# Reordering the head of a fused sketch-attention and routed expert kernel: pair numbers behind row scatters, batch 2's first work ahead of the first expert block

## Chip, cores and metric

The kernel runs on one core of a Trainium2 chip. The metric is the device time of one execution in microseconds (us), the median over the runs. A profile of one execution gives the durations. Five queues matter: PE (TensorE, with its weight loads shown as PEld), DVE (VectorE), ACT (ScalarE), POOL (GpSimd) and SP (SyncE, which here only issues transfers).

## What is computed

The reference has two stages. Attention with a polynomial sketch for 4 batches, 4 heads, 1088 tokens and head size 32, and then a mixture of 8 experts of which each of the 4352 tokens takes two.

```python
def phi(x):                                   # 64 features per head
    a = np.einsum('rd,bhsd->bhsr', S1, x)
    b = np.einsum('rd,bhsd->bhsr', S2, x)
    return np.einsum('bhsi,bhsj->bhsij', a, b).reshape(*x.shape[:-1], r * r)
q_p, k_p = (phi(q), phi(k))
kv = np.einsum('bhsf,bhsd->bhfd', k_p, v)     # state of a batch
z = np.sum(k_p, axis=2)
num = np.einsum('bhsf,bhfd->bhsd', q_p, kv)
den = np.einsum('bhsf,bhf->bhs', q_p, z)[..., None] + 1e-06
x = num / den                                 # then tokens x 128

logits = x @ w_gate
noisy_logits = logits + np.log1p(np.exp(x @ w_noise)) * noise
top2 = np.argpartition(-noisy_logits, 2, axis=1)[:, :2]
# softmax over the two, then for each expert e and rank k:
h = np.maximum(x[mask] @ w1[e], 0.0)          # 128 -> 1024
out[mask] += top2_w[mask, k, None] * (h @ w2[e])
```

## The kernel before

**Attention.** A batch is cut into 8 tiles of 128 tokens and a rest of 64 tokens; the rests of two batches share one tile. `Features` makes the 64 features of four tiles. `turn` transposes the inputs on PE and ACT copies them out (`xT`); `sketch` multiplies with the sketch on PE and ACT copies half of it out (`ab`); `multiply` is two DVE instructions, the second of which (`phi`, 1.23 us) is the outer product. `keys_values` accumulates the state `kv` of a batch over its key tiles in one PSUM bank; `through_router` passes that state through the gate weights (transposes, then a small product), so that the routing logits come out of the same product as the numerators. `Attend` transposes the query features (`phT`) and multiplies them with the state (`nd`).

**Routing.** `router` is a chain of some forty small DVE instructions for one batch (batch 0 is done in two halves, `h0` and `h1`, all later ones at once), with an exponential, a logarithm and another exponential on ACT in between. It ranks each token's two experts, counts with three small matmuls on PE (`side`, lines 564 to 566) how many pairs go before it, and ends with the row numbers `to` and with the rows `xg`, 128 values and one pair number each. The pair numbers are copied into `xg` by POOL (line 585); the 128 values are four DVE products (line 589). Then POOL sends the rows of 128 tokens at a time to a table in HBM (`xs`) by an indirect transfer (line 606): sixteen for batch 0, eighteen for batch 1. `xg` has two buffers. For batch 0 all rows are sent at once; later batches put theirs on a list (`waiting`), of which each expert block sends a few behind its own result.

**Expert blocks.** `table` works out on DVE which expert and which row each block of 128 pairs has: nine blocks from batch 0, then eighteen from batch 1, and so on, 72 in all with some spare at the end. `work_off` runs the blocks. SP loads a block's weights `w1` three blocks ahead and its rows `xb` two blocks ahead. The rows of a block wait for every scatter of the batches up to its own, and SP, PE, ACT, DVE and POOL each work their queue off in order. A block is a transpose of `xb` (line 767), eight matmuls into the hidden layer (line 821, ACT or DVE evict with the ReLU) and eight back (line 778, two half blocks later); POOL scatters the result (`parts`, line 785). The transpose of block b + 1 stands behind the first half of block b. At the end the two partial results of every token are summed.

**The order.** PE, ACT and DVE follow an order written out by hand (`tc.manual_schedule`); POOL and SP are ordered by the framework. `first_batches` does batches 0 and 1 up to batch 1's numerators, and batch 2's keys. Then generators alternate: for every half block the main loop takes one step of `routing` or `scores`, which hold what is left of the attention: `routing(1)` fills in batch 2's state, gate product and queries, `scores(2)` its numerators and batch 3's keys. `LONE` is the number of steps of `routing(1)` that run ahead of the first block.

PSUM is eight banks: three for features (`bank`), one for small things (`side`), two for the hidden layer (`hp`) and two for block results (`acc`). `early_bank` lets batches 0 and 1 use the last four as well, ahead of the blocks.

Of the kernel before, what the change touches and what calls it, by code (L numbers as in the profile page):

```python
# [21 lines left out]
def kernel(  # L22
# [310 lines left out]
    class Features:  # L333
# [7 lines left out]
        def turn(self):  # L341
            ps = early_bank(self.b, self.stream)
            for i, x in enumerate(self.tiles):
                nc.tensor.transpose(ps[:, P * i:P * (i + 1)], x, ident[:])  # L344
            self.xT = work.tile([P, 512], F32, name="xT", tag=f"xT{self.stream}")
            nc.scalar.copy(self.xT[:, 0:P * self.n], ps[:, 0:P * self.n])  # L346

        def sketch(self):
            n, ps = self.n, early_bank(self.b, self.stream)
# [63 lines left out]
        nc.scalar.copy(kv[RR:2 * RR, :, DH + 1:KC], both[RR:2 * RR, :, 2 * DH - 1:W])  # L413
        yield

    def through_router(b):

        kv = kvs[b]
        ps = early_bank(b, "k")
# [5 lines left out]
        ps = early_bank(b, "k")  # L425
# [48 lines left out]
    def router(nd, at_, n, t0, step, part, parts):  # L474
# [4 lines left out]
        def t3(name, w=E):  # L479
            return small.tile([P, MOST, w], F32, name=name, tag=name)[:, 0:n, :]  # L480
# [76 lines left out]
        if step == B - 1:  # L557
# [6 lines left out]
        nc.tensor.matmul(o, lhsT=earlier[:], rhs=at[0], start=True, stop=False)  # L564
        nc.tensor.matmul(o, lhsT=ones[:], rhs=so_far[:, NT - 1:NT - 1 + n, :], start=False, stop=False)
        nc.tensor.matmul(o, lhsT=ones[:], rhs=before[:].unsqueeze(1).to_broadcast([P, n, E]), start=False, stop=True)
# [5 lines left out]
        yield V.tensor_tensor(  # L572
            out=co[:, :, 0:n], in0=den.rearrange("p t a h -> p t (a h)").unsqueeze(1).to_broadcast([P, 2, n, H]),
            in1=g[:, :, 0:n].unsqueeze(3).to_broadcast([P, 2, n, H]), op=ALU.mult)
        row = t3("row")
        yield V.tensor_tensor(out=row, in0=o, in1=base[:].unsqueeze(1).to_broadcast([P, n, E]), op=ALU.add)
        of = small.tile([P, 2, MOST, E], F32, name="of", tag="of")[:, :, 0:n]
# [7 lines left out]
        nc.gpsimd.tensor_copy(xg[:, :, 0:n, D:XW].bitcast(I32), pair[:, :, t0:t0 + n].unsqueeze(3))  # L585

        for i in range(2):
            for hp in range(2):
# [7 lines left out]
                send(n)  # L596


    waiting = []

    ORDER = mybir.DependencyInfo(mybir.DependencyClass.NoSync, mybir.DependencyReason.SCHED_ONLY)

    def send(n, behind_=None):
        for _ in range(min(n, len(waiting))):
            step, i, t, to, xg = waiting.pop(0)
            x = nc.gpsimd.indirect_dma_start(  # L606
                out=xs[:], out_offset=bass.IndirectOffsetOnAxis(ap=to[:, i, t:t + 1], axis=0),
                in_=xg[:, i, t, :], in_offset=None)
            disjoint("xs", x, step)
            if behind_ is not None:  # L610
                tc.add_manual_dep(x.ins, behind_.ins.name, ORDER, reason="few at a time")

# [25 lines left out]
    def table(step, K, last):  # L638


        S_ = 3 * E if last else E
        ps = early_bank(step, "n") if step == 0 else side_bank()
        nc.tensor.matmul(ps[0:1, 0:E], lhsT=ones[:, 0:1], rhs=carry[-1][:], start=True, stop=True)
        both = const.tile([1, 2, E], F32, name=f"cnt{step}")
        if last:
# [94 lines left out]
    def work_off(*waves, skip=0, most=None, at=None):  # L740
# [68 lines left out]
            fetch_rows(i)  # L809
        acc = accumulator()  # L810
        turn_input(0, acc)
        for b in range(n):
# [58 lines left out]


    whole = slice(0, P)
    LONE = 2
    old_tokens = 3 * S - HALF
    mains = [load_batch(0)]
    load_rests(range(2), "kv")
# [32 lines left out]
    def all_of(steps_):  # L910
        for _ in steps_:
            pass
# [7 lines left out]
    def first_batches():  # L920
# [55 lines left out]
        both(8)  # L976
        p1.turn()
        p0.sketch()
        both(7)
        both(2)  # L980
        p1.sketch()
        both(3)
        all_of(h0)
        prepare(2)
        m0, m1, mr = key_parts[2]
        l0.multiply()
        m0.turn()
        l1.multiply()
        m1.turn()
        making = blocks_table(0)  # L990
        next(making)
        values = keys_values(1)
        next(values)
        next(values)
        next(values)
        all_of(h1)
        p0.multiply()
        columns = through_router(1)
        next(columns)
# [24 lines left out]

    def scores(b, nd):


        a = attends(b, nd)
# [6 lines left out]
        a[0].turn()  # L1035
        yield
        a[0].multiply()
        yield
        for f in nk:
            f.sketch()  # L1040
        for f in nk:
            f.multiply()
        yield
        a[1].turn()
        yield
        a[1].multiply()
        yield
        for x in a[2:]:
            x.turn()
            yield  # L1050
            x.multiply()
            yield

    def routing(b, nd):

# [15 lines left out]
                f.sketch()  # L1071
            yield

        filling = fill()
        for _ in steps_:
            some(steps_, 5)
            next(filling, None)
            yield
        for _ in filling:
            yield  # L1080
        making, features_ = blocks_table(b), products(nq)
        for _ in making:
            some(making, 7)
            some(features_, 2)
# [12 lines left out]
        return work_off(*[(b, WAVES[b], b > 1, WAVES[b]) if b < B - 1 else (b, LAST, True, OLD) for b in bs], **part)  # L1097

    with tc.manual_schedule(engines={PE, ACT, DVE}):
        nd = first_batches()  # L1100
        steps_ = routing(1, nd)
        some(steps_, LONE)
        needs = [0]
        blocks = block_work(*range(B), most=-SPARE, at=needs)

        def go_on():
            if needs[0] < len(tabs):
# [2 lines left out]
        for _ in steps_:  # L1110
            go_on()
        for b in (2, 3):
            nd = numerators()
            for x in (scores(b, nd), routing(b, nd)):
                for _ in x:
                    go_on()
        for _ in ends(tabs[-1], LAST):
# [45 lines left out]
```

## Time and profile before

| | us |
|---|---|
| median of 3 runs | 391.84 (390.15 to 396.99) |
| the profiled execution | 381.7 |
| its span, first to last instruction | 379.8 |
| PE busy | 352.2 (93%) |
| DVE busy | 153.7 (40%) |
| ACT busy | 126.0 (33%) |
| POOL busy | 153.3 (40%) |
| mean granted PE clock | 0.971 of full |

The profile's page gives busy time by engine and by fortieths of the span; the timelines give each instruction with its start, its length, and in brackets the idle time before it and what ended it. The profiled execution is shorter than the median of the timed runs, so sums over the profile are compared with its own 381.7 us.

### The profile page before, as it was taken

How to read it: one execution, taken by the hardware profiler on the slowest of the kernel's cores; microseconds unless marked ns; L12 is line 12 of the kernel's file. 1: busy time of each engine (PE TensorE's matmuls, PEld its weight loads, DVE VectorE, ACT ScalarE, POOL GpSimd, SP SyncE). 2: the span in 40 equal slices, each digit the busy share in tenths (PEclk: the TensorE clock that was granted, in tenths of full speed). 3: DMA queues.
4: the chain of work that ended last, by engine and by line, in shares of the span. 5: the costliest groups of instructions: out<-in, count | busy, mean ns of one | idle time of the engine just before them, and what ended most of it. 6: DMA issues, size and time to landing. Idle time of an engine off the chain costs nothing.

```text
span 379.8 us, 9206 instructions
## 1 busy us (share of the span) xinstructions
PE 352.2 (93%) x3022; PEld 344.2 (91%) x3022; DVE 153.7 (40%) x490; ACT 126.0 (33%) x310; POOL 153.3 (40%) x205
## 2 busy tenths in 40 slices
PE   8897883999999999999999999999999999998880
PEld 7886773999999999999999999999999999998880
DVE  5759849245364440287302232322223222343230
ACT  2353340355543555544442212222221222221210
POOL 7001854058762286564655546323232222322230
PEclk9998998599999999999999999999999999999995
DMA  6799672435416465466579766656465667898812
GB/s 187 192 306 292 187 239 68 131 99 171 157 49 205 130 184 166 139 198 152 179 193 291 215 183 211 179 183 187 163 205 164 187 173 257 297 263 245 254 46 89
DMA packets 45582, 70.38 MB, mean 185 GB/s; under 512 B 9939, under 2 KB 31060, under 8 KB 45536
## 3 DMA queue, kind: packets, MB, share of 16 engines
q1 hardware_dynamic: 40896, 60.76, 54.3%
q0 software_dynamic: 4480, 8.96, 6.7%
q8 instruction: 27, 0.44, 0.5%
q14 instruction: 19, 0.16, 0.1%
q10 hardware_dynamic: 160, 0.07, 0.1%
HBM read 57.99 MB, written 12.03 MB: 184 GB/s over the span
## 4 chain that ended last, share of the span: by engine, by line
PE 70%; DMA 15%; DVE 4%; issue 4%; POOL 4%; ACT 1%; SPq 1%; POOLq 0%; ACTq 0%
PE hp L821 29%; PE acc L778 28%; DMA parts<-y,xb 9%; POOL xs L606 3%; PE bank L407 2%; DMA xs<-xg,to 2%; PE bank L464 2%; PE acc L767 2%; PE bank L351 2%; DMA vld<-in_v_dram 2%; DMA xb<-xs 1%; POOL parts L785 1%; PE acc L464 1%; PE bank L447 1%; DMA two<-parts 1%
## 5 line engine op out<-in xcount | busy, mean ns | idle before, releaser
L821 PE MATMUL hp<-bT,w 128*128 128x128 f32 x1152 | 156.1, 279 | 1.1 <-PE acc L767 0.6
L778 PE MATMUL acc<-w,h 128*128 x1152 | 152.2, 275 | 0.0
L821 PEld LDWEIGHTS hp<-bT,w 128*128 128x128 f32 x1152 | 142.5, 195 | 2.4 <-PE acc L767 1.2
L778 PEld LDWEIGHTS acc<-w,h 128*128 128x128 f32 x1152 | 140.5, 193 | 0.0
L785 POOL DMA_INDIRECT parts<-y,xb x72 | 74.9, 1041 | 161.5 <-DVE y L736 87.3
L738 ACT ACTIVATE h<-hp 128x512 f32<-128x512 f32 x99 | 59.1, 597 | 149.4 <-PE hp L821 148.7
L606 POOL DMA_INDIRECT xs<-xg,to x68 | 70.7, 1040 | 49.3 <-DVE xg L589 29.0
L736 DVE TENSOR_SCALAR h<-hp 128x512 f32<-128x512 f32 x45 | 31.1, 692 | 121.8 <-PE hp L821 121.8
L738 ACT COPY bT<-acc 128x128 f32<-128x128 f32 x72 | 19.1, 265 | 30.8 <-PE acc L767 30.7
L767 PE MATMUL acc<-ident,xb 128*128 128x128 f32 x72 | 20.1, 279 | 6.8 <-DMA xb<-xs 6.8
L371 DVE TENSOR_TENSOR phi<-ab 128x1024 f32<-128x1024 f32 (+1 forms) x18 | 20.5, 1136 | 0.6
L736 DVE COPY y<-acc 128x128 f32<-128x128 f32 x45 | 13.1, 292 | 12.4 <-PE acc L778 12.4
L767 PEld LDWEIGHTS acc<-ident,xb 128*128 128x128 f32 x72 | 10.4, 145 | 7.5 <-DMA xb<-xs 5.6
L351 PE MATMUL bank<-sk,xT 128*128 128x128 f32 x102 | 13.8, 281 | 2.0 <-ACT xT L346 1.9
L407 PE MATMUL bank<-vld,phi 128*128 128x96 f32 x128 | 15.3, 275 | 0.0
L351 PEld LDWEIGHTS bank<-sk,xT 128*128 128x128 f32 x102 | 12.2, 191 | 3.2 <-ACT xT L346 2.8
L407 PEld LDWEIGHTS bank<-vld,phi 128*128 128x128 f32 x128 | 14.8, 192 | 0.0
L366 DVE TENSOR_TENSOR ab<-bank,ab 128x256 f32<-128x256 f32 (+1 forms) x15 | 5.6, 374 | 17.6 <-ACT ab L358 17.6
L489 DVE TENSOR_SCALAR den<-nd 128x16 f32<-128x16 f32 (+2 forms) x5 | 1.0, 206 | 25.1 <-ACT nd L467 25.0
L589 DVE TENSOR_TENSOR xg<-nd,co 128x256 f32<-128x256 f32 (+2 forms) x20 | 10.9, 607 | 0.6 <-issue 0.2
L346 ACT COPY xT<-bank 128x512 f32<-128x512 f32 (+1 forms) x15 | 7.5, 523 | 8.9 <-PE bank L344 6.6
L738 ACT COPY y<-acc 128x128 f32<-128x128 f32 x27 | 7.2, 265 | 7.6 <-PE acc L778 7.5
(184 smaller groups left out, 242.7 us busy)
## 6 DMA issues: line engine op xcount, KB each, us to landing
w<-in_moe_w_dram SPq DMA_DIRECT2D x72, 512.0 KB
xb<-xs SPq DMA_DIRECT2D x72, 64.5 KB
two<-parts SPq DMA_DIRECT2D x8, 512.0 KB
kld<-in_k_dram SPq DMA_DIRECT2D x4, 512.0 KB
qld<-in_q_dram SPq DMA_DIRECT2D x4, 512.0 KB
vld<-in_v_dram SPq DMA_DIRECT2D x8, 256.0 KB
out_dram<-two SPq DMA_DIRECT2D x8, 256.0 KB
parts<-y,xb POOLq DMA_INDIRECT x72, 3.4
```

Source lines behind the costliest of these rows:

```text
L351: nc.tensor.matmul(ps[:, P * i:P * (i + 1)], lhsT=self.xT[:, P * i:P * (i + 1)], rhs=sk[:].rearrange("p i h y -> p (i h y)"), start=True, ...
L371: yield V.tensor_tensor(out=self.phi[:, 0:n].rearrange("p t h (i j) -> p (t h) i j", i=R), in0=th[:, :, 0, :].unsqueeze(3).to_broadcast([P ...
L407: nc.tensor.matmul(ps[:, W * hp:W * (hp + 1)], lhsT=lhsT, rhs=rhs, start=(t == 0 and hp == 0), stop=(t == NT), skip_group_check=True)
L464: nc.tensor.matmul(ps[rows, c0:c0 + YC], lhsT=self.phT[hp][:, P * i + rows.start:P * i + rows.stop], rhs=kv[:, hp, :], start=True, stop=True)
L589: yield V.tensor_tensor(out=xg[:, i, 0:n, 2 * DH * hp:2 * DH * (hp + 1)].rearrange("p t (h d) -> p t h d", h=2), in0=x[:, :, hp, 0:2 * (DH ...
L606: x = nc.gpsimd.indirect_dma_start(out=xs[:], out_offset=bass.IndirectOffsetOnAxis(ap=to[:, i, t:t + 1], axis=0), in_=xg[:, i, t, :], in_o ...
L736: V.tensor_scalar_max(o, i, 0.0) if relu else V.tensor_copy(o, i)
L738: nc.scalar.activation(out=o, in_=i, func=AF.Relu) if relu else nc.scalar.copy(o, i)
L767: nc.tensor.transpose(acc[:, P:2 * P], rows[i][:, 0:D], ident[:])
L778: nc.tensor.matmul(acc[:, 0:D], lhsT=h[:, P * j:P * (j + 1)], rhs=w2[:, bass.ds(FJ * e + (j0 + j), 1), :], start=(j0 + j == 0), stop=(j0 + ...
L785: sent = nc.gpsimd.indirect_dma_start(out=parts[:], out_offset=bass.IndirectOffsetOnAxis(ap=rows.pop(i)[:, D:XW].bitcast(U32), axis=0), in ...
L821: nc.tensor.matmul(hp[:, P * j:P * (j + 1)], lhsT=w1[:, P * (j0 + j):P * (j0 + j + 1)], rhs=xT[:], start=True, stop=True)
```

## The change

In `router`, the copy of the pair numbers gets an ordering edge behind the last row scatter recorded so far (`sent_rows`), and for batches 1 to 3 the three counting matmuls are issued after the five DVE instructions that follow them. In `first_batches`, batch 2's keys are transposed earlier, in an `acc` bank; batch 1's state and gate product come ahead of the rest of `h1`; the first table comes later; and batch 2's state, gate product, both query groups and the first transposes of its numerators are issued before the first block. `through_router` can take its banks from another stream. The first table's counts use the `side` bank. After the first block's input transposes, the first numerator product of batch 2 is issued (`a.pop(0).multiply()`). `routing(1)` has no attention work left to fill in, apart from one query product, and `scores` is written as one loop. `LONE` becomes 1, since `first_batches` has already run a step of `routing(1)`.

```diff
@@ router @@
+        def rank_sums():
+            nc.tensor.matmul(o, lhsT=earlier[:], rhs=at[0], start=True, stop=False)
...
+        if step == 0:
+            rank_sums()
         yield V.tensor_add(out=after[:], in0=before[:], in1=so_far[:, NT + n - 1, :])
...
+        if step > 0:
+            rank_sums()
         row = t3("row")
...
-        nc.gpsimd.tensor_copy(xg[:, :, 0:n, D:XW].bitcast(I32), pair[:, :, t0:t0 + n].unsqueeze(3))
+        numbers = nc.gpsimd.tensor_copy(xg[:, :, 0:n, D:XW].bitcast(I32), pair[:, :, t0:t0 + n].unsqueeze(3))
+        if sent_rows:
+            tc.add_manual_dep(numbers.ins, sent_rows[-1].ins.name, ORDER, reason="rows first")
@@ table @@
-        ps = early_bank(step, "n") if step == 0 else side_bank()
+        ps = side_bank()
@@ work_off @@
         turn_input(0, acc)
+        yield
@@ first_batches @@
         p0.sketch()
+        prepare(2)
+        (m0, m1, mr), (n0, n1) = key_parts[2], query_parts[2]
+        m0.turn("n")
+        turning = m1.turning("n")
+        next(turning)
         both(7)
         both(2)
         p1.sketch()
         both(3)
+        all_of(turning)
         all_of(h0)
-        prepare(2)
-        m0, m1, mr = key_parts[2]
+        m0.sketch()
+        m1.sketch()
+        values = keys_values(1)
         l0.multiply()
-        m0.turn()
+        next(values)
         l1.multiply()
-        m1.turn()
-        making = blocks_table(0)
-        next(making)
-        values = keys_values(1)
         next(values)
         next(values)
-        next(values)
-        all_of(h1)
         p0.multiply()
-        columns = through_router(1)
-        next(columns)
-        some(making, 6)
-        p1.multiply()
-        m0.sketch()
         nd = numerators()
         a0, a1, ar = attends(1, nd)
+        columns = through_router(1, "q")
+        next(columns)
+        p1.multiply()
         a0.turn()
         next(columns)
         pr.turn()
+        all_of(h1)
+        a1.turn()
+        making = blocks_table(0)
+        next(making)
         pr.sketch()
-        some(making, 6)
-        a1.turn()
         a0.multiply()
         pr.multiply()
-        all_of(making)
+        m0.multiply()
         a1.multiply()
         ar.turn()
         ar.multiply()
-        m1.sketch()
+        all_of(making)
+        values = keys_values(2)
+        next(values)
         mr.turn()
+        n0.turn("q")
+        m1.multiply()
         mr.sketch()
-        m0.multiply()
-        m1.multiply()
+        n0.sketch("q")
+        next(values)
         mr.multiply()
-        return nd
+        n0.multiply()
+        steps_ = routing(1, nd)
+        next(steps_)
+        next(values)
+        n1.turn()
+        columns = through_router(2)
+        next(columns)
+        n1.sketch()
+        next(columns)
+        nd = numerators()
+        a = attends(2, nd)
+        a[0].turn()
+        return steps_, nd, a
@@ routing @@
-        filling = fill()
+        filling = fill() if b > 1 else iter(())
...
-        making, features_ = blocks_table(b), products(nq)
+        making, features_ = blocks_table(b), products(nq[1:] if b == 1 else nq)
@@ main @@
-        nd = first_batches()
-        steps_ = routing(1, nd)
+        steps_, nd, a = first_batches()
         some(steps_, LONE)
         needs = [0]
         blocks = block_work(*range(B), most=-SPARE, at=needs)
+        next(blocks)
+        a.pop(0).multiply()
```

More of the change, by code (lines that the diff above doesn't have):

```diff
@@ L339, in __init__, with bank, turn, turning @@
             self.n = len(tiles)
-        def turn(self):
-            ps = early_bank(self.b, self.stream)
+        def bank(self, stream=None):
+            return early_bank(*((self.b, self.stream) if stream is None else (0, stream)))
+        def turn(self, stream=None):
+            for _ in self.turning(stream):
+                pass
+        def turning(self, stream=None):
+            ps = self.bank(stream)
             for i, x in enumerate(self.tiles):
                 nc.tensor.transpose(ps[:, P * i:P * (i + 1)], x, ident[:])
+            yield
             self.xT = work.tile([P, 512], F32, name="xT", tag=f"xT{self.stream}")
             nc.scalar.copy(self.xT[:, 0:P * self.n], ps[:, 0:P * self.n])
-        def sketch(self):
-            n, ps = self.n, early_bank(self.b, self.stream)
+        def sketch(self, stream=None):
+            n, ps = self.n, self.bank(stream)
             for i in range(n):
@@ L414, in keys_values, with through_router @@
         yield
-    def through_router(b):
+    def through_router(b, stream="k"):
         kv = kvs[b]
-        ps = early_bank(b, "k")
+        ps = early_bank(b, stream)
         for hp in range(2):
@@ L424, in through_router @@
         yield
-        ps = early_bank(b, "k")
+        ps = early_bank(b, stream)
         for hp in range(2):
@@ L563, in router @@
         o = ps[:, 0:n * E].rearrange("p (i e) -> p i e", e=E)
-        nc.tensor.matmul(o, lhsT=earlier[:], rhs=at[0], start=True, stop=False)
-        nc.tensor.matmul(o, lhsT=ones[:], rhs=so_far[:, NT - 1:NT - 1 + n, :], start=False, stop=False)
-        nc.tensor.matmul(o, lhsT=ones[:], rhs=before[:].unsqueeze(1).to_broadcast([P, n, E]), start=False, stop=True)
+        def rank_sums():
+            nc.tensor.matmul(o, lhsT=earlier[:], rhs=at[0], start=True, stop=False)
+            nc.tensor.matmul(o, lhsT=ones[:], rhs=so_far[:, NT - 1:NT - 1 + n, :], start=False, stop=False)
+            nc.tensor.matmul(o, lhsT=ones[:], rhs=before[:].unsqueeze(1).to_broadcast([P, n, E]), start=False, stop=True)
+        if step == 0:
+            rank_sums()
         yield V.tensor_add(out=after[:], in0=before[:], in1=so_far[:, NT + n - 1, :])
@@ L596, in router @@
                 send(n)
-    waiting = []
+    waiting, sent_rows = [], []
     ORDER = mybir.DependencyInfo(mybir.DependencyClass.NoSync, mybir.DependencyReason.SCHED_ONLY)
@@ L609, in send @@
             disjoint("xs", x, step)
+            sent_rows.append(x)
             if behind_ is not None:
@@ L811, in work_off @@
         turn_input(0, acc)
+        yield
         for b in range(n):
@@ L873 @@
     whole = slice(0, P)
-    LONE = 2
+    LONE = 1
     old_tokens = 3 * S - HALF
@@ L1016, in first_batches, with scores @@
         ar.multiply()
-        m1.sketch()
+        all_of(making)
+        values = keys_values(2)
+        next(values)
         mr.turn()
+        n0.turn("q")
+        m1.multiply()
         mr.sketch()
-        m0.multiply()
-        m1.multiply()
+        n0.sketch("q")
+        next(values)
         mr.multiply()
-        return nd
-    def scores(b, nd):
-        a = attends(b, nd)
+        n0.multiply()
[11 more added lines that the diff above has]
+        return steps_, nd, a
+    def scores(b, nd, a):
         nk = []
@@ L1034, in scores @@
             f.turn()
[L1035 to L1048, printed above, removed]
+        for i, x in enumerate(a):
             x.turn()
@@ L1052, in scores @@
             yield
+            if not i:
+                for f in nk:
+                    f.sketch()
+                for f in nk:
+                    f.multiply()
+                yield
     def routing(b, nd):
@@ L1112 @@
         for b in (2, 3):
-            nd = numerators()
-            for x in (scores(b, nd), routing(b, nd)):
+            if b > 2:
+                nd = numerators()
+                a = attends(b, nd)
+            for x in (scores(b, nd, a), routing(b, nd)):
                 for _ in x:
```

## The prediction

> **What bounds the kernel now.** I read, in this order: the page (busy time and clock by slice), the table by stage, the timelines of GpSimd and TensorE over 47 to 80 us, then those of the DMA queue and TensorE at 114 to 117 us. From about 66 us to 360 us TensorE is busy almost without a break, so the end moves with whatever TensorE loses before and inside that stretch. The slices:
>
> ```profile
> PE   8897883999999999999999999999999999998880
> ...
> PEclk9998998599999999999999999999999999999995
> ```
>
> Slices 7 and 8 (57 to 76 us) hold the one large hole in the head: work falls, then the clock does. By stage (columns: window, then busy us of PE, PEld, DVE, ACT, POOL, granted clock, DMA share, GB/s):
>
> ```profile
> 60.00:65.00 5.00, 0.13 (x2) 0.00 (x0) 4.38 (x19) 0.52 (x2) 2.15 (x3) 0.93 0.16 51
> 65.00:70.00 5.00, 4.09 (x15) 3.30 (x16) 2.69 (x13) 1.16 (x4) 0.00 (x0) 0.50 0.50 148
> 70.00:75.00 5.00, 5.00 (x27) 4.94 (x27) 0.79 (x4) 1.82 (x6) 0.00 (x0) 0.55 0.40 114
> 75.00:80.00 5.00, 5.00 (x48) 5.00 (x47) 3.76 (x8) 2.56 (x7) 1.27 (x1) 1.00 0.33 93
> ```
>
> TensorE idles for five microseconds, then works ten at half clock: 27 instructions in 70 to 75, 48 in the next five. What it waits for stands in the timelines (start, length, instruction, in brackets the idle time before it and its releaser). GpSimd:
>
> ```profile
> 47.26 0.97 POOL L606 DMA_INDIRECT xs<-xg,to  x1 [0.30 <-issue]
> 50.86 0.51 POOL L585 COPY xg<-pair 128x18 int32<-128x18 int32 x1 [2.63 <-DMA xs<-xg,to]
> 51.61 0.98 POOL L606 DMA_INDIRECT xs<-xg,to  x1 [0.24 <-POOL xg L585]
> ...
> 61.28 0.97 POOL L606 DMA_INDIRECT xs<-xg,to  x1 [0.30 <-DMA xs<-xg,to]
> ```
>
> and TensorE:
>
> ```profile
> 56.42 3.71 PE L407 MATMUL bank<-vld,phi 128*128 128x96 f32 x32
> 65.55 0.48 PE L767 MATMUL acc<-ident,xb 128*128 128x128 f32 x1 [5.42 <-DMA xb<-xs]
> ```
>
> The first block needs sixteen row scatters, one every 1.27 us on GpSimd. Between the eighth and the ninth stands batch 1's copy of pair numbers, which waits until the first eight have been read out. TensorE runs dry at 60.13 and starts the block at 65.55 (call it T0). A second place matters more for this change. Block 9 is the first that needs batch 1's eighteen rows:
>
> ```profile
> 111.96 0.97 POOL L606 DMA_INDIRECT xs<-xg,to  x1 [0.30 <-DMA xs<-xg,to]
> 114.40 0.21 POOL L585 COPY xg<-pair 128x18 int32<-128x18 int32 x1 [1.48 <-DMA xs<-xg,to]
> ```
>
> ```profile
> 114.46 0.33 SPq L763 DMA_DIRECT2D xb<-xs  x1
> ```
>
> ```profile
> 115.53 1.06 PE L778 MATMUL acc<-w,h 128*128 x8
> 116.42 0.27 PE L767 MATMUL acc<-ident,xb 128*128 128x128 f32 x1
> ```
>
> The last scatter is issued at 111.96, has landed by 114.40, the load goes out at 114.46, and TensorE transposes those rows at 116.42 with no idle time shown. It is hidden, but with next to nothing to spare.
>
> **What the Trainium skill says.** "TensorE: Matmul & The Clock Gate", Part 1, has the clock at half after at least one idle window of about 3.4 us and back after a busy one. The trace agrees on the fall (half from 64.6 us), but the return took until 74.75, three such windows; and a dip to 0.50 at 34 to 37 us followed gaps of 1.3 us only. The same page (Architectural detail) has DVE, ACT and GpSimd as strict FIFOs, which is what the copy at 50.86 shows. "SBUF — State Buffer", SBUF: two separate sides, has DVE and GpSimd exclude each other on a shared port: the scatters that took 1.63, 1.84 and 1.73 us instead of 0.97 lie beside a DVE feature product of 1.23 us. "DMA: Bandwidth & Descriptors", Anatomy of one DMA, gives about 2 us plus bytes over 436 GB/s: 2.15 us estimated for 66 KB; the trace has 2.3 to 5.4.
>
> **The change, part by part** (before's clock throughout).
>
> *Pair numbers behind the scatters.* Batch 1's copy goes behind all sixteen; the second half's small copy (0.21) takes its place. The gap falls from 3.38 us to 0.30 + 0.21 + 0.24 = 0.75, so the sixteenth scatter, its landing and the first row load come 2.6 us earlier: T0 = 62.9. The first scatter stays at 36.53: it hangs on DVE, whose order up to there is unchanged. The second half's rows are now made after the two query products (2 x 1.6 us), at about 45.6 instead of 42.4; needed at 49, so free. The first table comes behind two feature products, at about 52 instead of 49.6; the three weight loads then go out near 53 and, at before's pace (issued 50.3, DMA all but idle at 58), land near 60.5. Free, with 2 us to spare. SP's order of transfers is unchanged. The counts for this table move to the side bank, which DVE frees at about 43.5 by reading the second half's rank sums; TensorE reaches them near 45.7, so this costs nothing. Were DVE late there, batch 1's numerators would queue behind it.
>
> *Batch 2 ahead of block 0.* TensorE work moved ahead of T0: rest values 0.58, state transposes 0.22, gate product 0.41, query transposes 0.87, sketches 1.79, first numerator transposes 0.87; together 4.74. Room: batch 2's key transposes (0.87) fall into the 1.33 us wait at 31.2, batch 1's numerators start about 2.3 us earlier, and 2.8 us are left between 60.1 and 62.9. Each hop waits for ACT or DVE (about 0.5 us); adding them up I have TensorE done near 62, so the hole shrinks from 5.4 us to about 1 and the clock should hold. That spares 9.2 us at 0.51, or 4.6 us.
>
> *What this uncovers.* From T0 to the tenth row transpose TensorE took 50.87 us. Less 4.6 of clock, less 4.74 moved, plus 0.80 (batch 3's rest values and state transposes, now ahead of it): 42.3, so it wants block 9's rows at 105.2. The rows don't shrink alike. Batch 1's rank sums now stand behind block 0's second half: 0.11 + 1.76 (moved numerator) + 4 x 0.89 + waits and the rest, 8.3 us after T0, at 71.2; from the rank sums' end to finished rows it was 4.15 us (75.87 to 80.02), so they are ready near 75.4 instead of 80.0. From there GpSimd is the bound: before, first to last scatter took 80.80 to 112.93, with five block results in between. Less 1.3 us that it waited for results, plus the copy of 0.45 that now stands inside: 31.3. So 75.8 + 31.3 = 107.1, landed 108.5, rows in SBUF 1.96 later: 110.5. TensorE waits 5.3 us there. Everything behind it in TensorE's queue waits too, and on SP the next weights stand behind this load; they have a block's time (3.7 us) to arrive, as now.
>
> *Sum.* The tenth transpose comes at 110.5 instead of 116.42, 5.9 us, and 0.8 us of work is behind it: 6.7. But the hole is as long as the one removed, so I expect the clock to fall again. Bounds: one window of 3.4 us at half costs 1.7; the first hole cost 4.6. I take 3.4 for it and 0.3 for a dip in the head: net 3.0. Elsewhere (tail, 320 us) nothing changes. The profiled execution took 381.7 us (span 379.8): 378.7. The timed runs lie higher, median 391.84; I carry the difference over: 388.8. A measurement of this kernel can tell about 2%, 7.8 us, from no change.
>
> Unknown costs: DVE's seventh large product beside the scatters, 0 to 0.8 us on T0; banks held by batch 2's second queries until their product, 0 to 1; the clock, 1.7 to 4.6. I take 0, 0 and 3.4. That gives 386.9 to 391.9 for this case alone.
>
> **Rivals.**
> - *The cover holds*: rows reach block 9 in time and both holes are gone. Gain 116.42 - 105.2 + 0.8 = 12.0: 379.8. For it: the rows start 4.6 us earlier. Against: eighteen scatters and five results at 1.27 each are 29 us by themselves.
> - *Block 0 isn't earlier*: batch 2's chain of hand-overs (keys, values, table, queries, numerators) ends only near 65.5, so the change doesn't do what it says at its first place. The rows shift along: 113.1 at the tenth transpose, gain 3.3 + 0.8 - 3.4 = 0.7: 391.1. For it: eleven hand-overs in one queue. Against: DVE and ACT are a third to two thirds busy there.
> - *Slower*: batch 1's exponential stands in ACT's queue behind batch 2's numerator copies, and its rank sums in TensorE's queue behind block 0. The tenth transpose is the row-ready time plus 35.1. It decides from 78.7 on (116.42 + 0.8 - 3.4 - 35.1): at 83 the kernel takes 396.1, and 2% slower needs 86.5. Against: I have 75.4, with DVE's chain (7 us from the exponential on) done at 70.
>
> **How the numbers follow.** Likeliest 0.62 (388.8), cover holds 0.12 (379.8), block 0 not earlier 0.15 (391.1), slower 0.11 (394 to 400). 382.5 to 394.5 holds the first, the third and half of the last. Faster by over 2%: the second and a little of the first, 0.15. Slower by over 2%: over half of the last and some of the third, 0.09. Within: 0.76.
>
> **What would show it.** Right: the ninth scatter 0.75 us behind the eighth's end; first block at 62 to 64 us at clock 1.0; a wait of 4 to 6 us of TensorE on row loads near 105 to 111, GpSimd without a gap before it, and a dip of the clock behind it. Wrong: no such wait (then near 380), or the first block past 65 us, or the clock at 1.00 right through the wait (then near 385).

## Result: 3.5% slower, where no change was forecast

The changed kernel took 405.31 us (median of 4 runs, 401.66 to 406.34); the kernel before took 394.28 us beside it (4 runs, 390.15 to 396.99). The ratio is 1.035, with a 95% interval of 1.026 to 1.044. Here and below, times are medians of all runs, while a ratio leaves out runs over 1.5% slower than the fastest of their kernel, so the two need not agree to the last digit. The forecast was 388.8 us with a range of 382.5 to 394.5, so it was wrong in sign and size. The profiled execution of the changed kernel took 406.34 us, its span is 404.6.

The page, same rows as shown of before:

```profile
PE   6988759999398998998999999999999999998980
...
PEclk9999755799899999899999999999999999998995
```

and the stages (columns as above):

```profile
60.00:65.00 5.00, 4.19 (x18) 3.78 (x18) 3.07 (x13) 1.92 (x5) 0.00 (x0) 0.50 0.31 112
65.00:70.00 5.00, 5.00 (x26) 4.47 (x26) 0.00 (x0) 0.59 (x2) 0.00 (x0) 0.50 0.85 258
70.00:75.00 5.00, 4.75 (x22) 4.46 (x22) 1.19 (x4) 1.34 (x4) 0.00 (x0) 0.50 0.30 107
75.00:80.00 5.00, 4.65 (x34) 3.99 (x34) 3.71 (x9) 1.54 (x5) 0.00 (x0) 0.93 0.00 0
```

TensorE is at half clock from about 45 to 76 us, not 65 to 75. GpSimd did what was forecast: the ninth scatter starts 0.48 us behind the eighth's end (forecast 0.75), and the sixteenth has left by 57.83, against 62.25 before:

```profile
46.49 0.97 POOL L623 DMA_INDIRECT xs<-xg,to  x1 [0.30 <-issue]
47.45 0.21 POOL L600 COPY xg<-pair 128x8 int32<-128x8 int32 x1
47.94 0.98 POOL L623 DMA_INDIRECT xs<-xg,to  x1 [0.28 <-POOL xg L600]
...
56.86 0.97 POOL L623 DMA_INDIRECT xs<-xg,to  x1 [0.30 <-issue]
```

But the first block starts at 81.00 instead of 62 to 64:

```profile
81.00 0.27 PE L785 MATMUL acc<-ident,xb 128*128 128x128 f32 x1
```

The loss is in the hand-overs from TensorE to ScalarE and VectorE. TensorE's timeline, then ScalarE's, then VectorE's:

```profile
48.54 1.91 PE L455 MATMUL acc<-ident,phi 128*128 128x128 f32 x8
50.38 0.20 PE L661 MATMUL side<-carry,ones 128*1 128x8 f32 x2
50.64 0.79 PE L359 MATMUL hp<-sk,xT 128*128 128x128 f32 x2
52.70 4.16 PE L472 MATMUL acc<-kv,phT 128*128 128x98 f32 x16 [1.27 <-issue]
```

```profile
52.06 0.58 ACT L460 COPY phT<-acc 128x512 f32<-128x512 f32 x1 [1.48 <-PE hp L359]
54.19 0.58 ACT L460 COPY phT<-acc 128x512 f32<-128x512 f32 x1 [1.54 <-remote]
56.33 0.21 ACT L366 COPY ab<-hp 128x64 f32<-128x64 f32 x1 [1.55 <-remote]
59.91 0.87 ACT L475 COPY nd<-acc 128x392 f32<-128x392 f32 x2 [3.37 <-remote]
```

```profile
54.23 0.15 DVE L668 COPY cnt<-side 1x8 f32<-1x8 f32 x1 [8.56 <-remote]
```

TensorE's transposes were done at 50.45, yet ScalarE copies the second half of them at 54.19; the counts were done at 50.58 and VectorE reads them at 54.23. "remote" and "issue" say that the profile found no signal in time. The trace's own record of TensorE's semaphore stands at 54.167, 0.02 us ahead of the copy: the engine didn't dawdle, the signal came late. In this stretch, while GpSimd sends, ScalarE steps on once per 2.13 us. The last send ends at 57.83, and ScalarE takes up the numerators 2.08 us behind it, at 59.91. The same holds in the other late traces of the changed kernel: ScalarE's next copy comes 2.09 to 2.24 us behind the end of the sixteenth send.

I measured this for every hand-over: for each ScalarE or VectorE instruction that waits for TensorE and comes out of idle time, its start minus the later of the matmul's end and its own engine's previous end. In the first profile of before, 341 such hand-overs have none over 0.11 us. In this one, 24 of 339 are over 0.3 us, the longest 4.63, and 22 of the 24 have a GpSimd send inside them. Below, an execution (or chip) with hand-overs over 0.3 us late is called late, one without them punctual. The first profile of before was of an execution without late signals (381.7 us); its timed runs (390 to 397) were not like it.

### The profile page after: what moved, and what is told of

Read it like the earlier page. It is cut to its first block, busy times and chain, and to the rows that moved or that the text cites. A ratio compares the mean times of both kernels' runs of the same rounds, so it can differ in the third digit from the quotient of the medians.

```text
span 404.6 us, 9203 instructions
## 1 busy us (share of the span) xinstructions
PE 364.5 (90%) x3022; PEld 353.5 (87%) x3022; DVE 153.2 (38%) x490; ACT 124.3 (31%) x310; POOL 150.4 (37%) x205
## 4 chain that ended last, share of the span: by engine, by line
PE 73%; DMA 12%; issue 5%; DVE 3%; ACT 3%; another core or an unknown queue 2%; POOL 1%; SPq 0%; POOLq 0%; ACTq 0%
PE hp L840 28%; PE acc L796 26%; DMA parts<-y,xb 8%; PE bank L415 5%; PE acc L472 2%; PE bank L472 2%; PE acc L785 2%; DMA vld<-in_v_dram 2%; PE acc L455 1%; PE bank L359 1%; PE hp L359 1%; DMA w<-in_moe_w_dram 1%; PE bank L455 1%; DMA two<-parts 1%
## 5 line engine op out<-in xcount | busy, mean ns | idle before, releaser
L796 PEld LDWEIGHTS acc<-w,h 128*128 128x128 f32 x1152 | 142.0, 194 | 1.7 <-issue 1.7
L623 POOL DMA_INDIRECT xs<-xg,to x68 | 67.9, 998 | 53.1 <-DVE xg L606 29.0
L415 PE MATMUL bank<-vld,phi 128*128 128x96 f32 x128 | 18.1, 304 | 0.4 <-DVE ab L374 0.4
L415 PEld LDWEIGHTS bank<-vld,phi 128*128 128x128 f32 x128 | 17.5, 220 | 0.8 <-DVE ab L374 0.6
L472 PE MATMUL acc<-kv,phT 128*128 128x98 f32 (+1 forms) x72 | 12.9, 358 | 5.4 <-ACT nd L475 3.6
L472 PEld LDWEIGHTS acc<-kv,phT 128*128 128x128 f32 (+1 forms) x72 | 11.6, 255 | 6.7 <-ACT nd L475 3.8
L785 PEld LDWEIGHTS acc<-ident,xb 128*128 128x128 f32 x72 | 10.3, 144 | 3.4 <-issue 1.7
L472 PE MATMUL bank<-kv,phT 128*128 128x98 f32 (+1 forms) x72 | 9.4, 280 | 2.5 <-ACT phT L460 1.6
L472 PEld LDWEIGHTS bank<-kv,phT 128*128 128x128 f32 (+1 forms) x72 | 8.0, 185 | 3.8 <-ACT phT L460 2.6
```

The source lines that it names most:

```text
L415: nc.tensor.matmul(ps[:, W * hp:W * (hp + 1)], lhsT=lhsT, rhs=rhs, start=(t == 0 and hp == 0), stop=(t == NT), skip_group_check=True)
L472: nc.tensor.matmul(ps[rows, c0:c0 + YC], lhsT=self.phT[hp][:, P * i + rows.start:P * i + rows.stop], rhs=kv[:, hp, :], start=True, stop=True)
L623: x = nc.gpsimd.indirect_dma_start(out=xs[:], out_offset=bass.IndirectOffsetOnAxis(ap=to[:, i, t:t + 1], axis=0), in_=xg[:, i, t, :], in_o ...
L785: nc.tensor.transpose(acc[:, P:2 * P], rows[i][:, 0:D], ident[:])
L796: nc.tensor.matmul(acc[:, 0:D], lhsT=h[:, P * j:P * (j + 1)], rhs=w2[:, bass.ds(FJ * e + (j0 + j), 1), :], start=(j0 + j == 0), stop=(j0 + ...
```

## Experiments

Five sets were run, each on one chip and in one session, beside before. The chip of the first comparison is not on record. On chip 1 signals are punctual, on chips 3, 6, 7 and 15 late. "First block" is TensorE's first row transpose.

### Both kernels again, and the change taken apart (chip 1)

Edge alone: old head with

```diff
+        numbers = nc.gpsimd.tensor_copy(xg[:, :, 0:n, D:XW].bitcast(I32), ...)
+        if sent_rows:
+            tc.add_manual_dep(numbers.ins, sent_rows[-1].ins.name, ORDER, reason="rows first")
...
```

(The rest of the edit makes the list `sent_rows` and fills it.)

No edge: the changed kernel with `if False:` in place of `if sent_rows:`. The other two are before and the changed kernel as they stand.

> The kernel before, once more, with its own profile. Three theories are carried through this set. BURST: the stalls of the changed kernel (instructions of ScalarE, VectorE and TensorE that start 1.5 to 8.5 us after their operands were made, while GpSimd issues its sixteen row scatters without a break) come from the unbroken burst of scatters, so from the ordering edge on the pair numbers. ORDER: they come from the new order of the head itself (batch 2's work and a late first table in front of the first block), whatever GpSimd does. CHANCE: they strike any version in some executions; the first profile of before (381.7 us, beside timed runs of 390 to 397) was one without them. BURST and ORDER expect here a time of 380 to 397 and no wait above 1.5 us of ScalarE or VectorE on a thing that was ready, with the first block's input transpose at 65 to 67 us. CHANCE expects 390 or more with such waits visible somewhere in 36 to 62 us or in 80 to 113 us, and the first block or the tenth transpose later than 65.6 and 116.4 by 3 us or more.

> The changed kernel once more. BURST and ORDER expect 400 to 407 us with the first block's transpose again at 78 to 84 us and TensorE at half clock from about 45 to 77. CHANCE expects the places of the stalls to move by several microseconds from one execution to the next, and the first block somewhere between 63 and 84.

> Before, with the ordering edge on the pair numbers alone: the sixteen scatters become one burst, nothing else of the order changes. BURST expects stalls in 48 to 58 us like those of the changed kernel, the first block at 70 us or later, and a time 5 to 12 us above before. ORDER expects the first block about 2.6 us earlier than in before (near 63), no stalls, and a time 0 to 3 us below before. CHANCE expects no difference from before beyond its spread (390 to 397).

> The changed kernel without the ordering edge: the pair numbers of batch 1 stand again between the eighth and the ninth scatter and wait there, the new order of the head stays. BURST expects no stalls, the first block at 64 to 67 us and a time of 385 to 394, level with before. ORDER expects the same stalls as in the changed kernel, the first block at 78 us or later, and 400 to 407. CHANCE expects about the changed kernel's median, with stalls in other places.

| chip 1, before 382.02 us | us | ratio (95%) |
|---|---|---|
| before again | 381.27 | 0.999 (0.996 to 1.002) |
| changed | 377.93 | 0.992 (0.989 to 0.995) |
| edge alone | 378.77 | 0.989 (0.983 to 0.994) |
| no edge | 383.97 | 1.006 (1.003 to 1.008) |

BURST, ORDER and CHANCE all failed on the changed kernel: it is a little faster than before, and no hand-over is over 0.11 us in any of the four traces, though 136 to 145 of them have a send inside. The page and the lines of the changed kernel on chip 1:

```profile
PE   8898898999959999999999999999999999997970
...
PEclk9999999999988999999999999999999999999996
```

```profile
46.03 0.20 PE L661 MATMUL side<-carry,ones 128*1 128x8 f32 x2
```

```profile
46.26 0.15 DVE L668 COPY cnt<-side 1x8 f32<-1x8 f32 x1 [0.57 <-PE side L661]
```

```profile
63.66 0.33 PE L785 MATMUL acc<-ident,xb 128*128 128x128 f32 x1 [0.90 <-DMA xb<-xs]
```

```profile
111.09 0.45 PE L785 MATMUL acc<-ident,xb 128*128 128x128 f32 x1 [4.37 <-DMA xb<-xs]
```

The same counts are read 0.04 us after TensorE's end, the first block comes at 63.66 at full clock, and TensorE waits 4.37 us for block 9's rows at 111.09. That is the forecast's picture. What separates the two comparisons isn't the kernel: before itself takes 382.02 us here and 394.28 there. I put it down to the chip, but each chip was measured in one session only, so chip and session can't be told apart.

### A second chip, and all of batch 1's rows at once (chip 3)

```diff
-            if step == 0:
+            if step <= 1:
                 send(n)
```

in the changed kernel and in the old head with the edge.

> The kernel before in a second session. Two theories of the difference between the first comparison (before 394.28, changed 405.31) and the second (382.02 and 377.93). SESSION: in the first comparison the completion signals of TensorE reached ScalarE and VectorE late (up to 5 us after the matmul) while GpSimd issued scatters, in every execution of that session, and the changed head suffers more since eleven hand-overs stand in front of its first block; whatever session has this is 8 us or more slower for before, and shows it in the trace. LOT: both comparisons drew from the same spread, and the changed kernel simply has two modes. SESSION expects either about 382 us with no late signal, or 390 to 397 us with late signals in 36 to 62 us or 80 to 113 us. LOT expects about 382 here whatever the changed kernel does.

> The changed kernel in a second session. SESSION expects it beside before as in one of the two comparisons: 376 to 381 us where before takes 379 to 385 (ratio 0.985 to 0.998, first block at 63 to 64 us), or above 400 where before takes 390 to 397. LOT expects single executions above 400 among others near 378, beside a before of about 382.

> The changed kernel with batch 1's eighteen row scatters sent at once, ahead of the block results on GpSimd's queue. In the second session's trace GpSimd needs from 77.45 to 107.64 for them, since a result of 1.3 us stands behind every third, and TensorE waits 4.37 us for block 9's rows and then runs 6.8 us at half clock. Theory GPSIMD (the queue of scatters is the bound there): the last scatter ends near 100.5, the rows land near 104, TensorE doesn't wait, and the time falls by 5 to 8 us against the changed kernel (370 to 373 beside 378). Rival ROWS (the rows are late by the routing chain or by the load, not by the queue): the wait stays above 3 us and the time within 2 us. Rival BACK (the delayed results fill up the eight result buffers or delay the last summing): the wait goes, but the time falls by less than 3 us or rises.

> The old head with the ordering edge and with batch 1's eighteen scatters sent at once. If the new order of the head is worth something only where GpSimd isn't the bound (GPSIMD), this takes 3 to 7 us more than the changed kernel with rows first, since the old head has its rows 3 us later and leaves the hole ahead of the first block: 374 to 379. If the head's order is worth nothing by itself (rival: its gain was the ordering edge's alone), both are within 2 us of each other.

Before took 394.69 us (395.48 over all its runs there), changed 401.68 (ratio 1.015, 1.010 to 1.021), rows first 412.99 (1.042, 1.034 to 1.049), the old head with rows first 412.54 (1.045, 1.037 to 1.054). SESSION held and LOT fell: the kernel before shows late signals too, 28 of 341, 24 of them with a send inside:

```profile
99.61 0.60 ACT L738 ACTIVATE h<-hp 128x512 f32<-128x512 f32 x1 [2.42 <-PE bank L351]
102.47 0.27 ACT L738 COPY bT<-acc 128x128 f32<-128x128 f32 x1 [2.27 <-PE hp L821]
```

The transpose for the second line ended at 96.73. GPSIMD couldn't be judged here: more unbroken sends meant more late signals, the longest 10.4 us in the old head with rows first.

### The two parts on a late chip, and sends that do nothing (chip 6)

```diff
+    for t in range(16):
+        disjoint("idle", nc.gpsimd.indirect_dma_start(
+            out=idle_rows[:], out_offset=bass.IndirectOffsetOnAxis(ap=idle_to[:, t:t + 1].bitcast(U32), axis=0),
+            in_=pad[:], in_offset=None))
```

> The old head with the ordering edge on the pair numbers alone. On a chip where TensorE's signals come on time (before near 382) it took 378.77, a ratio of 0.989, and should again (0.983 to 0.994). On a chip where they come late during GpSimd's sends (before near 395): theory BURST (the unbroken burst is what hurts: each hand-over that falls into it costs up to some microseconds) expects it slower than before there, ratio 1.00 to 1.015, with hand-overs over 1 us late in 48 to 60 us, where before has few. Rival LENGTH (what hurts is how many hand-overs stand in front of the first block, so the new order of the head) expects it at or below before, 0.985 to 1.000.

> The new head without the edge. On a chip with signals on time it took 383.97, a ratio of 1.0055, and should again. On a chip with late signals BURST expects it between before and the changed kernel, 1.000 to 1.010, since the break of 3.4 us between the eighth and the ninth scatter lets signals through; LENGTH expects it at the changed kernel's own ratio or above (1.015 to 1.025).

> The changed kernel with sixteen further row scatters at the start, of a constant tile into a table that nobody reads: they need nothing and run from about 8 to 28 us, while GpSimd would be idle; nothing else is changed. Theory SEND (GpSimd's sends delay TensorE's signals on the chips that have it, wherever they stand) expects hand-overs from TensorE to ScalarE or VectorE over 0.3 us late inside 8 to 28 us, where the changed kernel has none, and a time 2 to 8 us above the changed kernel's 401.7. Rival DATA (it is the rows' own traffic, the loads beside it or the routing that delay them) expects 8 to 28 us as before and a time within 2 us. On a chip with signals on time both expect no late hand-over and within 1 us of 378.

Beside a before of 392.28 us the edge alone took 397.85 (1.012, 1.001 to 1.024) and the new head without the edge 392.62 (1.001, 0.997 to 1.004). BURST held for both; LENGTH expected no loss from the edge and at least 1.015 without it. The edge's interval reaches down to 1.001, so against LENGTH the second result is the stronger one. The idle sends (406.97 us; the changed kernel had no run on this chip) ran from 8.00 to 30.64 and made hand-overs late where they never had been. TensorE, then ScalarE:

```profile
21.84 2.85 PE L472 MATMUL acc<-kv,phT 128*128 128x98 f32 x23
25.01 1.13 PE L472 MATMUL acc<-kv,phT 128*128 128x98 f32 x8 [0.33 <-issue]
```

```profile
28.06 0.49 ACT L475 COPY nd<-acc 128x392 f32<-128x392 f32 x1 [3.10 <-PE bank L351]
32.31 0.49 ACT L475 COPY nd<-acc 128x392 f32<-128x392 f32 x1 [3.77 <-remote]
```

The last product ended at 26.15; its copy starts at 32.31, and on chip 1 the corresponding copy starts at 25.58. These sends move a constant tile that nobody reads, so DATA falls: the sends make the signals late, whatever they carry. Whether it is GpSimd's issuing or the transfers that follow wasn't separated.

### The changed kernel, rows first and idle sends side by side (chip 15)

> The changed kernel as the partner of the next two on one chip. The theory (LATE: a chip either delivers TensorE's signals late during GpSimd's sends or doesn't) expects one of two pictures and nothing between: before near 382 with the changed kernel at 0.986 to 0.997 of it and no hand-over over 0.3 us, or before at 387 to 400 with the changed kernel at 1.010 to 1.045 and twenty or so hand-overs over 0.3 us. A rival (DRIFT: the lateness comes and goes on any chip) expects a mixture within this set.

> The changed kernel with batch 1's eighteen scatters ahead of the block results. On a chip with punctual signals GPSIMD (the queue of scatters bounds block 9's rows) expects the wait of 4.4 us gone and 370 to 374 us; its rival ROWS expects the wait to stay and 376 to 379. On a late chip LATE expects 406 to 417, 2 to 4% over the changed kernel, as the burst of eighteen catches the hand-overs of the first blocks.

> The changed kernel with sixteen sends of a constant tile at 8 to 28 us into a table that nobody reads. On a chip with punctual signals LATE expects no late hand-over in 8 to 36 us and the changed kernel's time within 1 us. On a late chip it expects two to six late ones of up to 4 us there, and 1 to 6 us over the changed kernel. DRIFT expects late ones on any chip.

A late chip again: before 395.08, changed 407.25 (1.033, 1.018 to 1.048), rows first 412.36 (1.051, 1.038 to 1.063), idle sends 411.96 (1.049, 1.031 to 1.066). In the idle sends' trace hand-overs at 25 to 33 us are 1.73, 3.82 and 2.64 us late; in the changed kernel's none ahead of 45 us. The 4.7 us between the two medians lie inside overlapping intervals, so the lateness is shown and its price is not. Rows first lies 1.3% above the changed kernel, less than the 2 to 4% that LATE expected. DRIFT found no support: every trace of this set is late, as every trace of chip 1's set is punctual. A slower drift, from session to session, isn't excluded.

### One hop moved (chip 7)

In every late trace of the changed kernel the counts of the first table are 3.7 to 6.7 us late. So they were moved ahead:

```diff
         p1.multiply()
+        all_of(h1)
+        making = blocks_table(0)
+        next(making)
         a0.turn()
         next(columns)
         pr.turn()
-        all_of(h1)
         a1.turn()
-        making = blocks_table(0)
-        next(making)
```

once with the edge and once without.

> The changed kernel as the partner of the other three. On a late chip 400 to 408 us and a first block at 78 to 84 us; on a punctual one 377 to 380 and 63 to 64.

> The changed kernel with one TensorE product moved: the first table's counts are taken ahead of batch 1's numerator transposes instead of behind them; no other queue changes. Theory HOP (on a late chip the hop of the counts is the costly one, since VectorE works in order and batch 1's and batch 2's feature products stand behind it) expects the copy of the counts at 45 to 49 us instead of 54 to 60, the first block 3 to 8 us earlier and the time 3 to 8 us lower than the changed kernel's. Rival QUEUE (TensorE's signals leave one after another, and whichever comes next in the burst is as late) expects the lateness to move to another hop and the time within 3 us. On a punctual chip both expect the changed kernel's time within 1.5 us.

> The same without the ordering edge, so with the break of 3.4 us between the eighth and the ninth scatter. On a late chip HOP expects the best of the new heads, 385 to 391 where before takes 390 to 396 (a ratio of 0.985 to 1.000); QUEUE expects what the new head without the edge took beside before, a ratio of 0.997 to 1.004. On a punctual chip both expect 382 to 385, as without the edge.

> The changed kernel with batch 1's eighteen scatters ahead of the block results. On a late chip 410 to 414 us, as twice already. On a punctual chip GPSIMD expects TensorE's wait of 4.4 us for block 9's rows to vanish and 370 to 374 us; its rival ROWS expects the wait to stay, at 376 to 379.

| chip 7, before 394.47 us | us | ratio (95%) | first block |
|---|---|---|---|
| changed | 402.75 | 1.026 (1.013 to 1.039) | 78.47 |
| counts early | 402.76 | 1.027 (1.016 to 1.037) | 78.95 |
| counts early, no edge | 394.12 | 1.002 (0.998 to 1.006) | 72.41 |
| rows first | 410.15 | 1.041 (1.029 to 1.053) | 80.84 |

HOP fell. VectorE now reads the counts at once, and nothing is gained: ScalarE's copy of the numerators starts at 59.37, and in the changed kernel on this chip at 59.40. Counts early, VectorE and ScalarE:

```profile
45.66 0.15 DVE L668 COPY cnt<-side 1x8 f32<-1x8 f32 x1 [0.50 <-PE side L661]
```

```profile
51.53 0.59 ACT L460 COPY phT<-acc 128x512 f32<-128x512 f32 x1 [1.52 <-PE hp L359]
53.66 0.59 ACT L460 COPY phT<-acc 128x512 f32<-128x512 f32 x1 [1.55 <-remote]
54.14 0.22 ACT L366 COPY ab<-hp 128x64 f32<-128x64 f32 x1
59.37 0.87 ACT L475 COPY nd<-acc 128x392 f32<-128x392 f32 x2 [5.01 <-remote]
```

The lateness passes to the next hop (5.01 us), as QUEUE said. Without the edge GpSimd sends nothing from 46.91 to 50.69, and ScalarE works through the same copies in and just behind that pause:

```profile
49.35 0.59 ACT L460 COPY phT<-acc 128x512 f32<-128x512 f32 x1 [0.29 <-PE acc L455]
50.20 0.59 ACT L460 COPY phT<-acc 128x512 f32<-128x512 f32 x1 [0.27 <-PE acc L455]
...
51.40 0.49 ACT L475 COPY nd<-acc 128x392 f32<-128x392 f32 x1 [0.50 <-PE acc L472]
```

So on one chip, with one edit, the edge costs 8.6 us by the medians (402.76 against 394.12) and about 10 by the ratios. Behind the pause the lateness is back: in the same trace a copy of numerators comes 5.4 us late, at 61.40. On chip 1 the edge is worth 6.0 us (383.97 against 377.93), there in the changed head with the counts in their place.

## Why the prediction was wrong

The runs compare heads as follows. Each entry is from one trace, all punctual ones of chip 1; the late ones are of chip 3 (before), chip 6 (edge alone, no edge) and, for the changed kernel, of the first comparison and chips 3, 7 and 15.

| | first block, punctual | first block, late | span, punctual | span, late |
|---|---|---|---|---|
| before | 64.49 | 68.33 | 376.2 | 393.0 |
| edge alone | 66.07 | 75.92 | 380.5 | 399.4 |
| no edge | 67.00 | 72.62 | 382.5 | 391.9 |
| changed | 63.66 | 78.47 to 82.51 | 375.5 | 399.5 to 406.1 |

The two steps that failed are the price of a hand-over and the carry-over to the timed runs, both below.

**The scatters** were right: forecast 0.75 us between eighth and ninth, measured 0.48 and 0.61.

**The first block** was forecast at 62.9. On chip 1 it is 63.66, with TensorE's hole 0.90 us (forecast about 1), at full clock, and the weights' loads issued at 52.82 (forecast near 53). In the late traces it is 78.5 to 82.5, past the 65 us that the forecast itself named as a sign of being wrong. The step that failed there is "Each hop waits for ACT or DVE (about 0.5 us)": in the changed kernel's late traces a hop beside a send comes up to 6.7 us late, and that delay is handed down TensorE's queue to the first block (81.00 in the first of them, 18.1 us behind the forecast). The clock goes down as well. In the first late trace it is at half from 44.93, inside a wait of 2.65 us of TensorE, to 75.65 us, and eight query transposes take 1.91 us instead of the 1.04 of chip 1:

```profile
45.06 1.04 PE L455 MATMUL acc<-ident,phi 128*128 128x128 f32 x8
```

**Block 9's rows** were right on chip 1: rows finished at 76.68 (forecast 75.4), last scatter done at 107.64 (107.1), tenth transpose at 111.09 (110.5), wait 4.37 (5.3). The clock dip behind it lasts 6.8 us at half, which is the 3.4 us that were taken for it. Scatters and results follow each other there at 0.30 us; that GpSimd's queue is the bound is read from this and wasn't shown by a run, since rows first met late chips three times.

**The sum** was 378.7 for the profiled execution; on chip 1 it took 377.26, and the median gain over before was 4.1 us (forecast 3.0). That agreement is partly luck. The hole of 5.42 us and the ten us at half clock that the sum removes belong to one execution of before. In the second punctual trace of before the hole is 1.82 us, the first block comes at 64.49 at full clock, the tenth transpose at 111.56, and the span is only 0.7 us above the changed kernel's. Two slips change nothing: the three unknown costs give 387.1 to 391.8, not 386.9 to 391.9, and the half-clock stretch of before lies at 64.25 to 74.49 in the trace's own record, not at 64.6 to 74.75.

**The carry-over** is where the number broke: "The timed runs lie higher, median 391.84; I carry the difference over". That 10.1 us was treated as a constant of the measurement. It goes with late signals, and it depends on the order of the work: from punctual to late the span of before grows by 16.8 us (376.2 to 393.0), that of the changed kernel by 29.1 (375.5 to 404.6). These are single executions. By the medians before takes 10.3 to 13.5 us more on the late chips than on chip 1, and the changed kernel 23.8 to 29.3. The difference, 12.3 us by the spans and 10 to 16 chip by chip, turns a gain of some 3 to 4 into a loss of 6 to 12 (6.2, 8.3 and 12.2 on chips 3, 7 and 15), and 11.0 was first measured. It arises ahead of the first block: 17.3 us there for the changed kernel (63.66 to 81.00), 3.8 for before (64.49 to 68.33).

**Why before suffers less.** From punctual to late the first block moves by 3.8 us in before, by 9.9 with the edge alone, by 5.6 with the new order alone and by 15 to 19 with both. The number of hops alone doesn't explain it: beside the second eight scatters I count 6 and 8 of them in the two punctual traces of before and 9 in the changed kernel's. On chip 7 the pause ahead of the ninth scatter, which the edge takes away, lets the waiting signals through, and with it the first block comes at 72.41 instead of 78.95. That the new order makes each delay dearer since batch 2's chain stands in front of the first block fits the table, but was only argued.

**The rivals.** "Block 0 isn't earlier" named the right place, but had it at 65.5 by ordinary hand-overs. "Slower" named ScalarE's exponential behind numerator copies; batch 1's first scatter follows the first block by 13.95 us in the late trace and 13.79 in the punctual one, so that queue added nothing. "Cover holds" didn't occur.

What stays open is why chips (or sessions) differ, whether recording has a part in it (last section), and where the edge alone gains its 1.1% on chip 1: its one trace is of its slowest execution. No version beats before on a late chip. The changed kernel's loss there is clear of zero on chips 3, 7 and 15, while only in the first comparison is its whole interval above 2%. On chip 1 the changed kernel and the edge alone beat it, by about 1%, and aren't told apart.

## What to carry to other kernels

When a profile is shorter than the timed runs, the gap is not a constant to be added: ask which waits the timed runs have that the profile lacks, and whether the edit puts more work in their way. A pause in one queue may be what another queue lives on; here a "wasted" 3.4 us of GpSimd was worth 8.6 us on one chip, and its removal gained 6.0 on another. Compare a change of this size on more than one chip before calling it a gain or a loss.

## What was unexpected in the hardware

- On four of five chips, each in one session, TensorE's signals came late while GpSimd sent rows, up to 6.7 us in the changed kernel and 10.4 in the old head with rows first; on the fifth no trace has it. Only TensorE's: some 35 hand-overs between ScalarE and VectorE, or from them to TensorE, stayed within 0.2 us in the same traces.
- In the first late trace the signals come through 2.13 us apart (ScalarE at 52.06, 54.19, 56.33), in the changed kernel's on chip 7 only 1.43 us (50.86, 52.29). The Trainium skill, "TensorE: Matmul & The Clock Gate", The cost: per-tile semaphore tail, says that when every tile's matmul increments a semaphore the increments serialize, at 26.3 ns each. The punctual traces, where no hop is over 0.11 us, don't contradict that. The late gaps are something else, and not one signal per 2.13 us either: behind one of them two of TensorE's signals stand 0.04 us apart (54.17 and 54.21).
- The late traces also hold fewer records: of landed transfers 3,512 to 3,772 against 5,700 to 5,720, of TensorE's own signals 397 to 420 against 466 to 470, of ScalarE's 237 to 259 against 296 to 298. That is why many late waits are labelled "remote" or "issue". Whether the two have one cause wasn't tried. So a rival stands untested: the recording could itself hold up signals and lose records. Every execution here comes with a span and a granted clock, so all were recorded in some form, and none shows the kernel without it.
